# A gated linear recurrence followed by a token and channel mixer: the two chunks of a later group taken one after the other, with another table of urgencies

## The chip, the cores and the metric

The kernel runs on one core of a Trainium2 chip. The metric is the device time of one execution in microseconds (us), and lower is better. The engines are called as the profile calls them: PE is TensorE (PEld is its loading of weights, which can overlap the products), DVE is VectorE, ACT is ScalarE, POOL is GpSimd and SP is SyncE. POOL and SP only issue transfers in the part of the program that matters here.

## The reference

Two blocks run one after the other. The first is a recurrence with complex gates, for 4 batches, 8 heads, 768 positions and a head size of 48. The second mixes over positions at rank 32 and then over channels with a hidden width of 1536. All data are float32.

```python
mag = np.sqrt(a_re * a_re + a_im * a_im)
scale = np.minimum(mag, 0.999) / (mag + 1e-06)
ar, ai = a_re * scale, a_im * scale
for t in range(S):                         # S = 768
    S_re, S_im = (ar_t * S_re - ai_t * S_im + k_t v_t^T,
                  ar_t * S_im + ai_t * S_re)
    y[:, :, t] = q_t @ S_re
x = y as (B, S, H*D)                       # (4, 768, 384)
h = x.transpose(0, 2, 1) @ U @ V           # U (768, 32), V (32, 768)
u = x + h.transpose(0, 2, 1)
out = u + np.maximum(u @ w_ch1, 0) @ w_ch2 # w_ch1 (384, 1536), w_ch2 (1536, 384)
```

## The kernel before, in words

**Chunks.** The 4 x 768 positions are cut into 24 chunks of 128 (six to a batch). `GROUPS` holds chunks 0 and 1 as groups of one and then eleven groups of two (`GC = 2`). The gates (magnitude, logarithm, phase, sine and cosine) are worked out for a whole group at a time by `gates`, mostly on ACT and DVE. For each chunk, `prep` weighs q and k, turns them by their phases and transposes them on PE (`tr`, L660) into the tile `QK`, which has 96 rows.

**The chain of a chunk.** `chain(i)` makes the 128x128 causal matrix of each of the 8 heads level by level. There are five small steps on PE: three times `inner` (L694: 32 matmuls in tiles of the array that are 96 rows by 32 columns), then `corners` (L743: 16 matmuls, 96x32) and `corner` (L760: 8 matmuls, 96x64). In float32 each of these is two records in the trace, so one `inner` step shows as x64. Between two steps DVE multiplies `QK` in place (`times` and `grow`, recorded at L312, 96x1024) by totals of the gates (`T`). After each `inner` step a masked copy (`keep`, L700, DVE) takes the diagonal blocks out of PSUM into `DG`; four transfers by SP place them in `AT` (L731). ACT copies the corners into `AT` (L748, L764). Then come the transposes of k (`ks`, L780), the outputs (`yT`, L794 and, for all but the first chunk of a batch, L798), the state (`dk`, L809) and the turn back (`yr`, L824). `tot` (L578, in `gates`) and `yT` also use the array in tiles that are narrower than 128 columns.

**The mixer.** After the sixth chunk of a batch, three mixers (12 in all, two chunks each) are added to the plan: `mixed` (L861), `uTp` (L868), six steps `up` of 6 matmuls with 256 columns (L880), and the products `down` (L947; L904 for mixer 0). Results leave by POOL's queue (L891), those of the last mixer by SP's.

**The order.** Nothing is issued where it is written. Every step is added to a `Plan` with an engine, a cost, a rank, and what it reads and writes. `Plan.order` then lists all steps by simulating the engines with these costs, and this one list fixes each engine's order of instructions. A step with the lowest urgency among those that are ready goes first. The urgency of the steps of chunk i is looked up in the table `URGENCY` (`prep`, `levels` for the first three steps, `rest` for what follows); the mixers' large products have `n + 1000` and so fill what is left over. `way=1` marks PE steps that use tiles of the array: the planner charges `change` (0.12) where PE goes from one kind to the other, and prefers a step of the same kind if its urgency is within `stay` (4.0). Before the first mixer's products the planner puts `spare` matmuls (L1067), whose result nobody reads, where PE has nothing to do.

**Pairs.** For groups from `PAIRED = 6` on (chunks 10 to 23, seven groups), `chunks(g)` prepares both chunks and then calls `together` with both chains. `chain` is a generator that yields its five small steps; `together` takes the next one of each chain and adds the two as one PE step with the sum of the costs, the urgency of the first chunk, the reads of both, and PSUM tiles and destinations of both. Such a step shows as inner x128 in the trace. The chains' other steps are added between these, each with its own urgency.

Of the kernel before, what the change touches and what calls it, by code (L numbers as in the profile page):

```python
# [22 lines left out]
BLK = 32  # L23

URGENCY = {
    "w1": {0: -34.77, 1: -91.94, 2: 138.23, 3: 260.09, 4: 568.49, 5: 287.6, 6: 296.57},
    "w2": {0: 650.7, 2: 523.09, 4: -249.29, 6: 129.92, 8: 543.42, 10: 182.29, 12: 94.19},
    "gates": {0: -78.45, 1: -71.5, 2: 78.63, 4: -234.27, 6: 143.18, 8: 215.64, 10: 30.99, 12: 47.49, 14: 142.08,
        16: 274.38, 18: 114.7, 20: -16.24, 22: 169.1},
    "angles": {0: -70.73, 1: -53.23, 2: -131.01, 4: 19.06, 6: -65.31, 8: 37.85, 10: -61.12, 12: -16.54, 14: -136.88,  # L30
        16: -195.15, 18: 196.11, 20: -175.82, 22: 226.2},
    "prep": {0: -170.41, 1: 140, 2: -141.91, 3: 258.54, 4: -14.67, 5: -36.16, 6: -99.41, 7: -276.32, 8: 64.29,
        9: 195.98, 10: -226.17, 11: -71.5, 12: -336.86, 13: -82.47, 14: 72.82, 15: -103.91, 16: 99.41, 17: 10.29,
        18: -125.03, 19: 313.53, 20: -42.62, 21: 390.29, 22: -13.68, 23: -202.37},
    "levels": {0: 25.49, 1: -241.92, 2: 189.55, 3: -76.47, 4: -144.22, 5: -38.31, 6: -47.77, 7: -81.78, 8: 73.09,
        9: -35.34, 10: 106.7, 11: -81.83, 12: 144.3, 13: -3.44, 14: 138.61, 15: 149.75, 16: -3.41, 17: -279.49,
        18: 131.44, 19: 484.09, 20: 212.52, 21: -233.89, 22: -120.03, 23: 283.09},
    "rest": {0: 147.76, 1: 132.91, 2: 111.2, 3: 94.14, 4: 79.58, 5: 43.3, 6: 213.4, 7: 72.05, 8: 69.08, 9: 53.84,
        10: 15.71, 11: 8.04, 12: 146.3, 13: 334.57, 14: 62.95, 15: 59.48, 16: -119.25, 17: -34.74, 18: 266.96,
        19: 135.14, 20: 205.81, 21: 22.53, 22: 320.65, 23: -217.03},  # L40
}


# [129 lines left out]
def kernel(  # L173
# [37 lines left out]
    NCH = S // CH  # L211
# [3 lines left out]
    MC = 2  # L215
# [3 lines left out]

    GROUPS = [(0, 1), (1, 2)] + [(n, n + GC) for n in range(2, NT, GC)]  # L220
    NG = len(GROUPS)

    PAIRED = 6

    SIZES = (4, 8, 16, 32, 64, 128)
    NTOT = CH // 2
# [21 lines left out]
    def buffer(base, tag, bufs, shape, space=None, padded=None):  # L248

        if tag not in pools:  # L250
            pools[tag] = pool(tag, bufs, **({"space": space} if space else {}))
        plan.buffer(base, tag, bufs, space is not None)
        kw = {"padded_shape": padded} if padded else {}
        makers[base] = lambda: pools[tag].tile(shape, FP, tag=tag, name=base[0], **kw)

    def ring(base, tag, tiles):

        plan.buffer(base, tag, len(tiles))
        n = plan.turn[base] % len(tiles)
        makers[base] = lambda: tiles[n]  # L260
# [19 lines left out]
    def c_dma(n):  # L280
        return n * 512 / 170e3


    def PE(*a, **kw):
        plan.add("PE", *a, late=0.17, **kw)
# [34 lines left out]
    def where(i):  # L320
        return divmod(i, NCH)
# [16 lines left out]
    w1 = singles.tile([128, KD, FF], FP, name="w1")  # L338
    w2 = singles.tile([128, KF, DM], FP, name="w2")
# [87 lines left out]
    def load_qkv(i):  # L427
        buffer(("qk", i), "qk", 2, [128, 2, H, D])
        ring(("VP", i), "VP", VP)
        for u, src in enumerate((q, k)):  # L430
            SP(c_dma(DM), ("load", (1.3, 2.5)[i] if i < 2 else i + 3.7), lambda u=u, src=src: nc.sync.dma_start(out=get("qk", i)[:, u], in_=rows(src, i)),
               writes=[("qk", i, u)])
        SP(c_dma(DM), ("load", (1.4, 2.6)[i] if i < 2 else i + 4), lambda: nc.sync.dma_start(out=get("VP", i)[:, :, 0:D], in_=rows(v, i)), writes=[("VP", i)])
# [205 lines left out]
    def prep(i):  # L639
        R1 = "prep", i  # L640
        g = group_of(i)
        qk, QK = ("qk", i), ("QK", i)
        buffer(QK, "QK", 3, [D2, 2, H, CH])
        def weigh():
            a = get(*qk).rearrange("p u h d -> p u (h d)")
            mul(a, a, get("es", i))
        DVE(c_dve(2 * DM), R1, weigh, [("es", i)], [qk])
        for u in range(2):
            qkc = ("qkc", 2 * i + u)
            buffer(qkc, "qkc", 1, [128, H, 2, D])  # L650
            DVE(c_dve(2 * DM), R1, lambda u=u, qkc=qkc: mul(
                get(*qkc), get(*qk)[:, u].unsqueeze(2).to_broadcast([128, H, 2, D]), get("cs", g)[:, i - GROUPS[g][0]]),
                [qk, ("cs", g)], [qkc])
            for hh in range(2):
                ps = ("tr", (i, u, hh))
                psum(ps, "T", [128, HH, CH])

                def turn(qkc=qkc, hh=hh, ps=ps):
                    for j in range(HH):
                        nc.tensor.transpose(out=get(*ps)[0:D2, j], in_=get(*qkc)[:, hh * HH + j].rearrange("p u d -> p (u d)"),  # L660
                                            identity=ident)
                PE(0.44, R1, turn, [qkc], [ps], takes=[QK])
                ACT(c_act(HH * CH) - 0.05, R1, lambda u=u, hh=hh, ps=ps: nc.scalar.copy(  # L663
                    out=get(*QK)[:, u, hh * HH:(hh + 1) * HH], in_=get(*ps)[0:D2]), [ps], [QK + ((u, hh),)])
# [3 lines left out]
    def chain(i):  # L668
        c = where(i)[1]
        RL, RR = ("levels", i), ("rest", i)  # L670
        QK, DGi, ATi, VPi = ("QK", i), ("DG", i), ("AT", i), ("VP", i)
# [9 lines left out]
        def inner(n, hf):  # L681

            def part(a, p):
                return a if hf < 8 else a.rearrange(p + " (b x t) -> " + p + " b x t", x=2, t=hf)[..., 1, :]

            w = BLK if hf < 8 else BLK // 2
            ps = ("inner", (i, n))
            psum(ps, "A", [128, H, w], [128, 512 // w, w])

            def products():  # L690
                for h in range(H):
                    for j in range(CH // BLK):
                        js = slice(j * BLK, (j + 1) * BLK)
                        nc.tensor.matmul(out=get(*ps)[js, h], lhsT=k_of(h)[:, js], rhs=part(q_of(h)[:, js], "p"), start=True,  # L694
                                         stop=True, tile_position=(0, j * BLK))
            yield 0.6, RL, products, [QK], ps, DGi

            def keep():
                to, a = part(get(*DGi), "p h"), get(*ps)
                nc.vector.copy_predicated(out=to, mask=part(mask[:, n], "p").unsqueeze(1).to_broadcast(list(to.shape)),  # L700
                                          data=a if hf < 8 else a.rearrange("p h (b t) -> p h b t", t=hf))
            DVE(0.17 + 0.00104 * H * w, RL, keep, [ps, ("mask", 0)], [DGi])
# [15 lines left out]

            times(rank, hf, 2 * hf, hf, H * CH - hf, 0, u0, u1)

        yield from inner(5, 2)


        times(RL, 4, 16, 8, H * CH - 8, 0)
        yield from inner(1, 8)
        times(RL, 4, 16, 0, H * CH + 8, 2)
        grow(RL, 8)
        yield from inner(0, 16)
        for j in range(CH // BLK):
            js = slice(j * BLK, (j + 1) * BLK)  # L730
            SP(0.65, ("place", i), lambda js=js: nc.sync.dma_start(out=get(*ATi)[js, :, js], in_=get(*DGi)[js]), [DGi],  # L731
# [3 lines left out]
        ps1 = ("corners", i)  # L735
        psum(ps1, "A", [128, HH, BLK], [128, 4 * HH, BLK])

        def corners():
            for p in range(HH):
                for u in range(2):  # L740
                    for r in (0, 64):
                        h, to = 2 * p + u, r + u * BLK
                        nc.tensor.matmul(out=get(*ps1)[to:to + BLK, p], lhsT=k_of(h)[:, r:r + BLK],  # L743
                                         rhs=q_of(h)[:, r + BLK:r + 2 * BLK], start=True, stop=True, tile_position=(0, to))
        yield 0.4, RR, corners, [QK], ps1, ATi
        for r in (0, 64):
            for u in range(2):
                ACT(0.32, RR, lambda r=r, u=u: nc.scalar.copy(  # L748
# [4 lines left out]
        ps2 = ("corner", i)  # L753
        psum(ps2, "A", [128, HH, 64], [128, H, 64])

        def corner():
            for p in range(HH):
                for u in range(2):
                    h = 2 * p + u
                    nc.tensor.matmul(out=get(*ps2)[u * 64:(u + 1) * 64, p], lhsT=k_of(h)[:, 0:64], rhs=q_of(h)[:, 64:128],  # L760
                                     start=True, stop=True, tile_position=(0, u * 64))
        yield 0.5, RR, corner, [QK], ps2, ATi
        for u in range(2):
            ACT(0.37, RR, lambda u=u: nc.scalar.copy(  # L764
                out=get(*ATi).rearrange("p (a u) t -> p a u t", u=2)[0:64, :, u, 64:128], in_=get(*ps2)[u * 64:(u + 1) * 64]),
# [4 lines left out]
        if c < NCH - 1:  # L770
# [3 lines left out]
            for hh in range(2):  # L774
                ps = ("ks ps", (i, hh))
# [24 lines left out]
        for p0 in (0, 2):  # L800
            PE(0.95 if c else 0.5, RR, lambda p0=p0: outputs(p0), [VPi, ATi, QK] + ([("G", i - 1)] if c else []), [y + (p0,)], way=1,
               takes=[yTs])
# [203 lines left out]
    weights()  # L1006
    exps, trigs = "natural_log_exp_and_others", "trig_and_small"

    def together(chains):

        while True:
            at = [next(c, None) for c in chains]
            if at[0] is None:
                break
            cost, rank, f, reads, ps, to = zip(*at)
            PE(sum(cost), rank[0], lambda f=f: [x() for x in f], sum(reads, []), list(ps), way=1, takes=list(to))

    def chunks(g):
        both = list(range(*GROUPS[g]))
        for these in [both] if g >= PAIRED else [[i] for i in both]:  # L1020
            for i in these:
                load_qkv(i)
                prep(i)
            together([chain(i) for i in these])
            for i in these:
                if where(i)[1] == NCH - 1:
                    for m in range(i // MC - NCH // MC + 1, i // MC + 1):
                        mixer(m)


    waits, later, done = [], [], 0
    for g in range(NG):
        load_a(g)
        magnitudes, totals, turns, waves = gates(g)
        rank = "gates", GROUPS[g][0]
# [87 lines left out]
```

## Time and profile before

| | us |
|---|---|
| Median of 12 runs | 726.68 |
| Lowest and highest of them | 724.42, 728.17 |
| The profiled execution's own time | 727.8 |
| Its span, first to last instruction | 726.0 |

| engine | busy us | share of the span | instructions |
|---|---|---|---|
| PE | 707.7 | 97% | 10322 |
| PEld | 616.2 | 85% | 10322 |
| DVE | 484.0 | 67% | 732 |
| ACT | 399.3 | 55% | 734 |
| POOL | 49.8 | 7% | 91 |

The profiled execution's time is 1.8 us longer than its span and 1.1 us above the median of the runs. Matmuls are pipelined: each takes longer than the distance from its start to the start of the next, so that busy times of PE overlap, and the cost of a matmul to its successors is read from starts. `spare` makes up 58.5 us of PE's busy time.

### The profile page before, as it was taken

What the parts mean: (1) busy time and instruction counts of PE and PEld (TensorE: products, weight loads), DVE (VectorE), ACT (ScalarE), POOL (GpSimd) and SP (SyncE); (2) the same over time, 40 slices, a digit from 0 to 9 for tenths busy, and PEclk for the clock granted to TensorE, in tenths of its full rate; (3) what the DMA queues carried; (4) which work ended last, traced back from release to release, by engine and by line L of the source; (5) the groups of instructions that cost most, each with busy time, mean ns of one, the idle gap of its engine ahead of it and who ended that gap; (6) DMA issues with size and microseconds to landing.
All of it is one profiled execution on the core that took longest, in us unless ns stands there. A gap on an engine that the chain in (4) does not pass through costs nothing.

```text
span 726.0 us, 23175 instructions
## 1 busy us (share of the span) xinstructions
PE 707.7 (97%) x10322; PEld 616.2 (85%) x10322; DVE 484.0 (67%) x732; ACT 399.3 (55%) x734; POOL 49.8 (7%) x91
## 2 busy tenths in 40 slices
PE   7899998999999999999999999999999999999998
PEld 7777888786778888988888888798899898989997
DVE  5898999787997957878587686295684641322313
ACT  6695977857789686669988636514314122010010
POOL 5010000010100100000010001000000000000000
PEclk9999999999999999999999999999999999999999
DMA  8787854687415323253441042212110000000000
GB/s 204 154 210 145 203 105 81 136 197 129 101 32 115 67 60 65 43 106 63 84 96 23 17 91 55 45 30 44 34 38 14 13 28 1 22 1 23 6 16 23
DMA packets 165251, 53.00 MB, mean 73 GB/s; under 512 B 154080, under 2 KB 160416, under 8 KB 165152
## 3 DMA queue, kind: packets, MB, share of 16 engines
q1 hardware_dynamic: 161072, 42.26, 27.1%
q0 software_dynamic: 4080, 9.27, 5.5%
q8 instruction: 81, 1.33, 0.8%
q14 instruction: 18, 0.15, 0.1%
HBM read 33.59 MB, written 4.72 MB: 53 GB/s over the span
## 4 chain that ended last, share of the span: by engine, by line
PE 75%; ACT 11%; DVE 9%; issue 3%; DMA 1%; DVEq 0%; ACTq 0%
PE up L880 21%; PE down L947 19%; PE inner L694 5%; PE tr L660 5%; PE dk L809 3%; PE yT L794 3%; DVE QK L312 3%; ACT x L309 2%; PE down L904 2%; PE yT L798 2%; PE es ps L552 2%; PE mixed L861 2%; PE tot L578 2%; ACT y L309 1%; PE spare L1067 1%
## 5 line engine op out<-in xcount | busy, mean ns | idle before, releaser
L880 PE MATMUL up<-uT,w 128*128 128x256 f32 x864 | 196.1, 382 | 0.0
L312 DVE TENSOR_TENSOR QK<-QK,T 96x1024 f32<-96x1024 f32 x144 | 169.6, 1185 | 17.5 <-PE corners L743 7.2
L880 PEld LDWEIGHTS up<-uT,w 128*128 128x128 f32 x864 | 161.3, 190 | 22.8 <-issue 0.8
L309 ACT ACTIVATE h<-up 128x512 f32<-128x512 f32 x72 | 42.7, 594 | 158.2 <-PE up L880 155.6
L947 PE MATMUL down<-w,h 128*128 128x192 f32 x396 | 71.8, 327 | 0.0
L947 PEld LDWEIGHTS down<-w,h 128*128 128x128 f32 x396 | 65.2, 190 | 3.3
L312 DVE TENSOR_TENSOR qkc<-qk,cs 128x768 f32<-128x768 f32 x48 | 45.8, 953 | 30.2 <-PE tr L660 24.9
L939 DVE TENSOR_TENSOR stage<-h 128x384 f32<-128x384 f32 x22 | 12.2, 555 | 75.9 <-ACT h L309 75.9
L1067 PE MATMUL spare<-ident 128*128 128x128 f32 x404 | 58.5, 292 | 3.3 <-issue 1.9
L663 ACT COPY QK<-tr 96x512 f32<-96x512 f32 x96 | 52.1, 582 | 14.7 <-PE tr L660 14.5
L694 PEld LDWEIGHTS inner<-QK 96*32 96x32 f32 x4608 | 45.2, 109 | 17.4 <-issue 10.5
L1067 PEld LDWEIGHTS spare<-ident 128*128 128x128 f32 x404 | 52.4, 202 | 6.5 <-issue 2.7
L315 DVE TENSOR_TENSOR xo<-down,xo 128x192 f32<-128x192 f32 (+1 forms) x79 | 29.5, 385 | 38.2 <-PE down L947 38.2
L660 PE MATMUL tr<-ident,qkc 128*96 128x128 f32 x384 | 52.7, 275 | 2.0 <-DVE qkc L312 1.1
L694 PE MATMUL inner<-QK 96*32 96x16 f32 (+1 forms) x4608 | 50.7, 190 | 3.5 <-issue 2.8
L660 PEld LDWEIGHTS tr<-ident,qkc 128*96 128x96 f32 x384 | 41.3, 127 | 8.3 <-issue 1.8
L748 ACT COPY AT<-corners 32x128 f32<-32x128 f32 x96 | 24.5, 256 | 32.1 <-PE corners L743 31.0
L891 POOL DMA_DIRECT2D out_dram<-xo x32 | 17.9, 560 | 335.8 <-DVE xo L315 316.0
L700 DVE COPY_PREDICATED DG<-mask,inner 128x128 f32<-128x128 int32 (+1 forms) x72 | 24.2, 339 | 19.3 <-PE inner L694 19.0
L794 PE MATMUL yT<-AT,VP 128*64 128x128 f32 x384 | 36.8, 279 | 0.0
L947 PE MATMUL down<-stage 128*128 128x192 f32 x198 | 36.4, 327 | 0.0
L306 ACT ACT_TABLE_LOAD x26 | 33.4, 1283 | 1.2 <-PEq L1107 0.7
(116 smaller groups left out, 1106.7 us busy)
## 6 DMA issues: line engine op xcount, KB each, us to landing
stage<-in_moe_w_ch_dram SPq DMA_DIRECT2D x12, 768.0 KB, 5.1
ar<-in_a_re_dram SPq DMA_DIRECT2D x24, 192.0 KB, 3.4
ai<-in_a_im_dram SPq DMA_DIRECT2D x24, 192.0 KB, 3.7
qk<-in_q_dram SPq DMA_DIRECT2D x24, 192.0 KB, 3.3
qk<-in_k_dram SPq DMA_DIRECT2D x24, 192.0 KB, 4.4
VP<-in_v_dram SPq DMA_DIRECT2D x24, 192.0 KB, 3.2
w<-stage POOLq DMA_DIRECT2D x12, 384.0 KB, 6.6
T<-E SPq DMA_DIRECT2D x44, 96.0 KB, 3.2
```

The source lines that it names most:

```text
L306: ACT(1.37, rank, lambda: nc.scalar.preload_act_table_set(name), writes=[TABLE])
L309: return nc.scalar.activation(out=o, in_=i, func=f, **kw)
L312: nc.vector.tensor_tensor(out=o, in0=a, in1=b, op=OP.mult)
L315: nc.vector.tensor_tensor(out=o, in0=a, in1=b, op=OP.add)
L660: nc.tensor.transpose(out=get(*ps)[0:D2, j], in_=get(*qkc)[:, hh * HH + j].rearrange("p u d -> p (u d)"), identity=ident)
L663: ACT(c_act(HH * CH) - 0.05, R1, lambda u=u, hh=hh, ps=ps: nc.scalar.copy(out=get(*QK)[:, u, hh * HH:(hh + 1) * HH], in_=get(*ps)[0:D2]), ...
L694: nc.tensor.matmul(out=get(*ps)[js, h], lhsT=k_of(h)[:, js], rhs=part(q_of(h)[:, js], "p"), start=True, stop=True, tile_position=(0, j * BLK))
L748: ACT(0.32, RR, lambda r=r, u=u: nc.scalar.copy(out=get(*ATi).rearrange("p (a u) t -> p a u t", u=2)[r:r + BLK, :, u, r + BLK:r + 2 * BLK] ...
L794: nc.tensor.matmul(out=a[u * DP:(u + 1) * DP, p], lhsT=vv[:, h], rhs=get(*ATi)[:, h], start=True, stop=(c == 0), tile_position=(0, u * DP))
L880: nc.tensor.matmul(out=get(*ps)[:, e], lhsT=w1[:, f, (ff + e) * 128:(ff + e + 1) * 128], rhs=get(*uT)[:, f], start=(f == 0), stop=(f == KD ...
L947: nc.tensor.matmul(out=get(*to)[:, part], lhsT=x(j), rhs=y[:, j], start=(first and j == 0), stop=(j == KH - 1), skip_group_check=not first)
L1067: nc.tensor.matmul(out=spare[0], lhsT=ident, rhs=ident, start=True, stop=True)
```

## The change

The pairs are taken out: `PAIRED` and `together` go, `chain` adds each of its five small steps by itself, as a PE step with its own urgency, and `chunks` goes through the chunks of a group one after the other. For groups 2 to 5 that is what was done before, since there `together` had one chain. All seven tables in `URGENCY` have other numbers. The instructions that are issued are the same ones in kind and number; their order changes.

```diff
 URGENCY = {
-    "w1": {0: -34.77, 1: -91.94, 2: 138.23, 3: 260.09, 4: 568.49, 5: 287.6, 6: 296.57},
+    "w1": {0: 95.68, 1: -114.1, 2: 119.35, 3: 318.09, 4: 584.75, 5: 240.49, 6: 274.57},
...
-    "levels": {0: 25.49, 1: -241.92, 2: 189.55, 3: -76.47, 4: -144.22, 5: -38.31, 6: -47.77, 7: -81.78, 8: 73.09,
+    "levels": {0: 36.28, 1: -163.69, 2: 90.75, 3: -118.68, 4: -103.74, 5: 8.67, 6: -52.01, 7: -23.82, 8: 96, 9: 43.86,
...
-    PAIRED = 6
-
...
-            yield 0.6, RL, products, [QK], ps, DGi
+            PE(0.6, RL, products, [QK], [ps], way=1, takes=[DGi])
...
-        yield from inner(5, 2)
+        inner(5, 2)
...
-        yield from inner(1, 8)
+        inner(1, 8)
...
-        yield from inner(0, 16)
+        inner(0, 16)
...
-        yield 0.4, RR, corners, [QK], ps1, ATi
+        PE(0.4, RR, corners, [QK], [ps1], way=1, takes=[ATi])
...
-        yield 0.5, RR, corner, [QK], ps2, ATi
+        PE(0.5, RR, corner, [QK], [ps2], way=1, takes=[ATi])
...
-    def together(chains):
-
-        while True:
-            at = [next(c, None) for c in chains]
-            if at[0] is None:
-                break
-            cost, rank, f, reads, ps, to = zip(*at)
-            PE(sum(cost), rank[0], lambda f=f: [x() for x in f], sum(reads, []), list(ps), way=1, takes=list(to))
-
     def chunks(g):
-        both = list(range(*GROUPS[g]))
-        for these in [both] if g >= PAIRED else [[i] for i in both]:
-            for i in these:
-                load_qkv(i)
-                prep(i)
-            together([chain(i) for i in these])
-            for i in these:
-                if where(i)[1] == NCH - 1:
-                    for m in range(i // MC - NCH // MC + 1, i // MC + 1):
-                        mixer(m)
+        for i in range(*GROUPS[g]):
+            load_qkv(i)
+            prep(i)
+            chain(i)
+            if where(i)[1] == NCH - 1:
+                for m in range(i // MC - NCH // MC + 1, i // MC + 1):
+                    mixer(m)
```

More of the change, by code (lines that the diff above doesn't have):

```diff
@@ L25 @@
 URGENCY = {
-    "w1": {0: -34.77, 1: -91.94, 2: 138.23, 3: 260.09, 4: 568.49, 5: 287.6, 6: 296.57},
[L27 to L31, printed above, removed]
@@ L32 @@
-    "prep": {0: -170.41, 1: 140, 2: -141.91, 3: 258.54, 4: -14.67, 5: -36.16, 6: -99.41, 7: -276.32, 8: 64.29,
-        9: 195.98, 10: -226.17, 11: -71.5, 12: -336.86, 13: -82.47, 14: 72.82, 15: -103.91, 16: 99.41, 17: 10.29,
-        18: -125.03, 19: 313.53, 20: -42.62, 21: 390.29, 22: -13.68, 23: -202.37},
-    "levels": {0: 25.49, 1: -241.92, 2: 189.55, 3: -76.47, 4: -144.22, 5: -38.31, 6: -47.77, 7: -81.78, 8: 73.09,
-        9: -35.34, 10: 106.7, 11: -81.83, 12: 144.3, 13: -3.44, 14: 138.61, 15: 149.75, 16: -3.41, 17: -279.49,
-        18: 131.44, 19: 484.09, 20: 212.52, 21: -233.89, 22: -120.03, 23: 283.09},
@@ L38 @@
-    "rest": {0: 147.76, 1: 132.91, 2: 111.2, 3: 94.14, 4: 79.58, 5: 43.3, 6: 213.4, 7: 72.05, 8: 69.08, 9: 53.84,
-        10: 15.71, 11: 8.04, 12: 146.3, 13: 334.57, 14: 62.95, 15: 59.48, 16: -119.25, 17: -34.74, 18: 266.96,
-        19: 135.14, 20: 205.81, 21: 22.53, 22: 320.65, 23: -217.03},
+    "w1": {0: 95.68, 1: -114.1, 2: 119.35, 3: 318.09, 4: 584.75, 5: 240.49, 6: 274.57},
+    "w2": {0: 491.44, 2: 430.31, 4: -244.92, 6: 252.33, 8: 503.62, 10: 122.04, 12: 198.27},
+    "gates": {0: -36.9, 1: -11.04, 2: 97.92, 4: -176.1, 6: 172.63, 8: 170.19, 10: 39.76, 12: 33.76, 14: 86.36,
+        16: 212.52, 18: 142.25, 20: -14.92, 22: 119.88},
@@ new lines @@
+    "angles": {0: -48.49, 1: -68.04, 2: -149.7, 4: 26.37, 6: -18.74, 8: 27.33, 10: 2.93, 12: -18.2, 14: -106.29,
+        16: -135.42, 18: 99.1, 20: -223.01, 22: 213.99},
+    "prep": {0: -120.66, 1: 125.67, 2: -144.48, 3: 213.93, 4: -34.4, 5: 6.43, 6: -98.93, 7: -166.15, 8: 67.48,
+        9: 198.22, 10: -212.51, 11: 47.76, 12: -241.36, 13: -15.05, 14: 36.41, 15: -84.27, 16: 57.48, 17: 29.52,
+        18: -106.17, 19: 297.29, 20: 8.87, 21: 340.29, 22: 15.55, 23: -177.02},
+    "levels": {0: 36.28, 1: -163.69, 2: 90.75, 3: -118.68, 4: -103.74, 5: 8.67, 6: -52.01, 7: -23.82, 8: 96, 9: 43.86,
+        10: 78.26, 11: -98.96, 12: 174.48, 13: 49.88, 14: 84.4, 15: 102.2, 16: 22.96, 17: -168.27, 18: 153.18,
+        19: 552.85, 20: 149.19, 21: -218.14, 22: -98.92, 23: 245.11},
@@ L41 @@
+    "rest": {0: 160.12, 1: 84.71, 2: 92.21, 3: 84.11, 4: 44.14, 5: 13.55, 6: 221.57, 7: 36.88, 8: 6.37, 9: 42.74,
+        10: 3.06, 11: -2.44, 12: 170.29, 13: 268.3, 14: 86.43, 15: 53.53, 16: -130.49, 17: -80.04, 18: 187.27,
+        19: 178.6, 20: 234.63, 21: 84.11, 22: 252.98, 23: -194.62},
 }
```

## The prediction

> **What bounds the kernel now.** I read the page first, then busy time by stretch, then PE's waits, and last PE's instructions in order of time.
>
> ```profile
> PE 707.7 (97%) x10322; PEld 616.2 (85%) x10322; DVE 484.0 (67%) x732; ACT 399.3 (55%) x734; POOL 49.8 (7%) x91
> ...
> PE   7899998999999999999999999999999999999998
> ...
> PEclk9999999999999999999999999999999999999999
> ```
>
> PE is busy in nearly all of every slice but the first two, at its full clock. A busy PE may still hide slack, so the next view matters more: each row below is a stretch, its length, and the busy time of PE, PEld, DVE, ACT and POOL.
>
> ```profile
> 0.00:145.00 145.00, 132.74 (x2449) 113.90 (x2450) 125.60 (x186) 110.62 (x203) 16.56 (x40) 0.99 0.70 155
> ...
> 181.00:300.00 119.00, 117.53 (x2171) 100.22 (x2171) 100.04 (x139) 91.95 (x168) 8.68 (x13) 1.00 0.35 74
> 300.00:400.00 100.00, 99.62 (x1605) 86.19 (x1605) 73.93 (x109) 82.69 (x139) 6.40 (x10) 1.00 0.33 69
> 400.00:500.00 100.00, 98.99 (x1628) 86.92 (x1628) 66.09 (x99) 44.85 (x97) 5.77 (x9) 1.00 0.23 49
> 500.00:606.00 106.00, 106.00 (x1666) 95.59 (x1665) 58.83 (x93) 30.60 (x72) 3.24 (x6) 1.00 0.11 24
> 606.00:726.00 120.00, 116.77 (x634) 106.98 (x632) 31.77 (x70) 13.76 (x24) 4.86 (x9) 1.00 0.04 14
> ```
>
> Until 145 us DVE and ACT feed a PE that fills its gaps with spare matmuls. From 181 to 606 us PE stands idle for 119.00 - 117.53, 0.38, 1.01 and 0 us: 2.9 us in 425. From 606 us on only mixer products are left. So the end is set by the sum of PE's work; DVE, the next busiest, has 19 of 119 us free in its worst stretch and 47 of 106 in the last. PE's waits from 181 us on say the same (total, times, longest):
>
> ```profile
> PE inner L694 <- issue: 1.6, 3, 0.7
> PE tr L660 <- DVE qkc L312: 0.9, 1, 0.9
> PE uTp L868 <- DVE xo L315: 0.2, 1, 0.2
> ```
>
> No paired step is seen to wait for a chunk that is late. Something that shortens waits has 2.9 us to win; something that lengthens PE's own work is paid in full.
>
> **The instructions** are the same in kind and number: 5519 on PE in both built orders, 202 spares among them, 734 on DVE, 736 on ACT. The change's description speaks also of seven down products, of two banks and of last outputs by SP; both kernels have these, and the last 67 rows of PE's built order are equal. What remains is order. PE's first 200 rows are equal too, and row 200 stands at 181 us, so the start on PE is carried over. On DVE the first difference is a masked copy (0.29 us) set ahead of a multiplication at 90 us, on ACT a swap of two squares at 175 us. I take them at 0; the spares cover the first, and without that cover it is worth 0.3 us either way.
>
> **What a visit to the tiles costs.** In this view (start, duration, line, operation, number of records) starts count, since durations overlap:
>
> ```profile
> 476.13 1.14 PE L947 MATMUL down<-w,h 128*128 128x192 f32 x6
> 477.20 1.30 PE L694 MATMUL inner<-QK 96*32 96x16 f32 x128
> 478.43 1.08 PE L660 MATMUL tr<-ident,qkc 128*96 128x128 f32 x8
> 479.34 1.14 PE L947 MATMUL down<-w,h 128*128 128x192 f32 x6
> 480.32 2.11 PE L947 MATMUL down<-stage,h 128*128 128x192 f32 x12
> ```
>
> Six down records followed by more of them take 480.32 - 479.34 = 0.98 us; the six before the pair's inner step take 477.20 - 476.13 = 1.07. Going to the tiles costs 0.09. The joint step takes 478.43 - 477.20 = 1.23 for 128 records. A step of one chunk:
>
> ```profile
> 196.23 0.81 PE L552 MATMUL es ps<-GL,mid 128*128 128x384 f32 x2
> 196.96 0.69 PE L578 MATMUL tot<-total,GL 128*64 128x64 f32 x16
> 197.58 0.74 PE L694 MATMUL inner<-QK 96*32 96x16 f32 x64
> 198.25 0.69 PE L578 MATMUL tot<-total,GL 128*64 128x64 f32 x16
> ```
>
> It takes 198.25 - 197.58 = 0.67. Two of them make 1.34, or 0.11 over the joint step: that is the price of leaving a tile shape once, here for another shape (128x64), and the joint step's own exit to the full array is inside its 1.23. So a visit that is split in two pays 0.09 + 0.11 = 0.20 more.
>
> **How many.** The change dissolves 35 joint steps (7 groups, 5 steps) into 70. If each stood alone this would cost 35 x 0.20 = 7.0 us. The planner keeps tiled steps together when their urgencies lie close, so I counted in the built orders from PE's row 200 on, leaving out the alternation inside yT, which is the same in both. Stretches of tiled steps: 66 before, 76 after. Changes from one tiled kind of step to another inside a stretch: 18 before, 42 after (inner next to tot, corner next to inner, yT next to inner, each of another chunk). So 10 x 0.20 = 2.0 us for stretches, and 24 changes of shape. For these the view has 0.11 (inner to tot); between yT and inner it is up to 0.20, and between two shapes of equal width about 0.05. Most of the 24 have inner on one side, so I take 0.10: 2.4 us, with 1.2 and 4.8 as ends. Sum: 4.4 us more of PE's own time, from 3.2 to 6.8.
>
> On this the Trainium skill has a rule that speaks against the change: TensorEngine Tiling (Array Packing), section Key Properties, says that a change of tiling mode drains TensorE and that a change of tile within a mode does not. TensorE: Matmul & The Clock Gate, section Single matmul latency, gives a matmul's fixed part as 398 cycles, 166 ns at full clock; as an estimate, a full drain at each of the 44 changes would be 7.3 us, giving 734.0. The rows show about 0.1 us per change, and they decide.
>
> **Waits.** Gone with the pairs is the demand that both chunks' QK be ready, and the run of 128 small matmuls in which the trace has its gaps of issue (1.6 us in three; one of them, though, inside a step of one chunk). All of the 2.9 us is the most that this can give back. New is closeness. I added up PE's work between successive steps of one chunk in both orders. A step's products end, DVE makes the masked copy (0.34 to 0.45 us) and the multiplication of QK (1.19), then the next step may start: 1.6 us at least, and twice the DVE work for a pair. After 181 us the order before has one distance under 2.2 us; its pairs have at least 3.1 for corners to corner, and 4 to 11 between inner steps. The order after has eleven under 2.2 (1.2 to 2.2 us), three of them before 300 us, where DVE is 84% busy. The PE instruction queue stops at such a step, and all the mixer products queued behind it stop too. A DVE step of 0.55 to 0.95 us queued ahead would make each late by up to about 0.45 us: 0 to 5 us. I set this against the gaps given back and take 0 for the sum of both, from -2.9 to +5.0.
>
> **Queues that are moved past.** On SP, four transfers that place DG now stand between the four transfers of T at several places, so T waits for a masked copy; on POOL three or four z transfers come in a row, behind outputs that wait for DVE. T feeds the multiplications, z the phase product (ph), and ph has no wait after 181 us in the list above. I count nothing; uncovered, it adds to the same 0 to 5 us. After the last small tiled step both built orders have the same 117 us of mixer products (by row durations), so the end is unchanged.
>
> **The sum.** The profiled execution's 727.8 us + 4.4 + 0 = 732.2 us. That execution lies 1.1 us above the median of the runs, so the median to expect is 731.1.
>
> **Rivals.**
> *Coupling given back (faster).* Each chunk goes ahead when its own QK is ready, and PE's idle time after 181 us vanishes. With the changes of tiling at no cost this is 726.7 - 2.9 = 723.8 us. It decides if a change costs under 0.04 us (44 x 0.04 = 1.8, leaving a gain of 1.1). The views speak against it: paired steps are not seen waiting for data, and every change costs 0.09 or more. With the changes at the low end, 3.2 - 2.9, it lands at 727.0, which counts as no change.
> *Closeness (slower still).* All eleven near steps wait: 731.1 + 5.0 = 736.1, more if a late T or z adds. For it: DVE's 84%. Against: near distances lie beyond 300 us too, where DVE has 26% or more free.
> *PE has slack.* PEld is 85% busy, and then 4 us would vanish: 726.7. The Trainium skill, in Perfetto Trace Analysis, section Identifying the Most-Contended Engine, takes that share and not matmul busy time as the measure of headroom; by it some 110 us would be open. Against it stands the down step above: 0.98 / 6 = 0.163 us from start to start with nothing waited for; its weights load ahead.
>
> **How the numbers follow.** About 0.2% (1.5 us) is what a measurement of this kernel can tell from no change. The forecast (729 to 734 us) has 0.62; closeness or dearer changes (over 734) 0.22; waits given back or slack, 728.1 to 729 us, 0.03; within 725.2 to 728.1, 0.09; faster 0.04. So slower 0.87, same 0.09, faster 0.04. The range 727.0 to 735.5 leaves out the free changes below and the fullest closeness above.
>
> **What would show it.** Right: records of spare unchanged at 404, up starting near 145.6 us, inner as x64 in more visits with 0.67 us each, PE's idle time after 181 us near 3 us, and the mixer-only end starting 4 us later, near 610 us. Wrong: PE waits on DVE QK of several us (closeness), on ph (queues), an earlier start of the end stretch (coupling), or a start that moved before 181 us.

## The result, and the profile after

The kernel after takes 729.91 us (median of 12 runs, 728.06 to 731.76), the kernel before 726.51 us in the runs beside it. The ratio is 1.0046, with a 95% interval from 1.0033 to 1.0059: slower by 0.46%, or 3.4 us. The profiled execution after took 729.9 us and has a span of 728.0 us, 2.0 us more than the span shown before.

Busy times on the page of the kernel after:

```profile
PE 711.9 (98%) x10322; PEld 618.1 (85%) x10322; DVE 484.3 (67%) x732; ACT 399.7 (55%) x734; POOL 49.5 (7%) x91
```

The work is the same and PE is busy 4.2 us longer. The stretches (length, then the busy time of PE, PEld, DVE, ACT, POOL) say where:

```profile
0.00:145.00 145.00, 133.11 (x2450) 113.97 (x2451) 125.86 (x186) 111.24 (x203) 16.59 (x40) 0.99 0.70 156
...
181.00:300.00 119.00, 118.76 (x2206) 101.52 (x2205) 102.06 (x139) 94.84 (x173) 7.56 (x11) 1.00 0.36 74
300.00:400.00 100.00, 99.63 (x1870) 85.20 (x1870) 79.88 (x117) 75.96 (x138) 5.85 (x9) 1.00 0.38 78
400.00:500.00 100.00, 99.89 (x1787) 86.44 (x1776) 72.42 (x104) 54.28 (x107) 4.80 (x7) 1.00 0.21 43
500.00:606.00 106.00, 106.00 (x1199) 96.06 (x1199) 44.55 (x77) 24.64 (x56) 4.86 (x9) 1.00 0.08 20
```

The start is as it was. From 181 to 606 us PE stands idle for 0.24 + 0.37 + 0.11 + 0 = 0.7 us, where it was 2.9. PE's waits from 181 us on are these two:

```profile
PE ph L608 <- ACT QK L661: 0.2, 1, 0.2
PE tr L658 <- ACT x L307: 0.2, 1, 0.2
```

So PE waits less and still ends later, with the same work: it has become slower at it. PE in order of time (start, duration), after:

```profile
301.65 0.62 PE L822 MATMUL yr<-ident,yTs 128*128 128x128 f32 x4
302.20 0.76 PE L692 MATMUL inner<-QK 96*32 96x32 f32 x64
302.89 1.08 PE L658 MATMUL tr<-ident,qkc 128*96 128x128 f32 x8
...
306.80 1.31 PE L692 MATMUL inner<-QK 96*32 96x32 f32 x128
308.04 1.56 PE L550 MATMUL es ps<-GL,mid 128*128 128x384 f32 x4
```

An inner step of one chunk alone takes 0.69 us; where the planner sets two side by side (x128), they take 1.24 together.

**A ledger of PE's time.** I added up the distances from one start to the next of all PE records in each trace, from the first up to the last record. A *change* is a passage between the full array, tiles of 64 columns (corner, tot, yT) and tiles of 32 (inner, corners, rank); its price is what the distance has over the step's own spacing. In all traces the medians are the same: 0.093 us from the full array to either width, 0.095 to 0.100 from 64 columns to the full array or to 32, 0.104 to 0.117 from 32 to 64 or to the full array, and nothing between two steps of the same width, though one has 96 rows and the other 128. A second cost sits behind it: after an exit to the full array the second record, too, comes late, by 0.104 us (up, down, ph, mixed) or 0.035 to 0.057 (transposes, dk). *Waits* are distances over 0.15 us beyond all that.

| kernel | changes | first up to end, us | changes, us | second records | waits | rest |
|---|---|---|---|---|---|---|
| before | 154 | 576.8 | 15.6 | 5.7 | 4.4 | 551.2 |
| after | 189 | 579.2 | 19.4 | 6.4 | 2.1 | 551.3 |
| before_again | 154 | 576.0 | 15.6 | 5.6 | 3.6 | 551.2 |
| after_again | 189 | 578.7 | 19.4 | 6.4 | 1.5 | 551.4 |
| pairs_other_table | 154 | 585.9 | 15.6 | 6.0 | 11.1 | 553.2 |
| single_old_table | 202 | 586.1 | 20.4 | 7.1 | 6.2 | 552.5 |
| full_ahead | 161 | 583.8 | 16.3 | 6.3 | 2.5 | 551.0 + 7.8 |
| full_between | 224 | 593.6 | 22.8 | 9.2 | 2.5 | 551.3 + 7.8 |
| shifted | 154 | 581.3 | 15.6 | 5.7 | 8.8 | 551.2 |
| after_shifted | 189 | 578.6 | 19.4 | 6.4 | 1.6 | 551.4 |
| single_fewer | 173 | 578.6 | 17.2 | 6.4 | 3.2 | 551.8 |
| fewer_changes | 141 | 572.4 | 13.9 | 5.5 | 2.5 | 550.5 |

The rest, PE's own work, is equal to 0.2 us between before and after. The change adds 3.8 us of changes and 0.7 us of second records and gives back 2.3 us of waits (2.1 by the second pair of profiles). From the first up to the end the two pairs of traces differ by 2.4 and 2.7 us, of the measured 3.4.

Up to 1 us is not in the ledger, and the granted clock is the likely place of it. In both first traces the clock is halved for 3.4 us, at 60.1 us before and at 59.6 us after; in the second pair it is full throughout up to the last product, and the first up comes 2.8 and 2.3 us sooner. All 12 runs of the kernel after have a clock of 0.995 to 0.999. The 49 runs of the kernel before beside the experiments have 1.000 in 19 cases, with a median of 725.1 us, and 0.998 or less in 29, with 727.3. Against the latter the kernel after is 2.6 us slower, as in the ledger; that this is the whole of it isn't shown.

### The profile page after: what moved, and what is told of

Read it like the earlier page. It is cut to its first block, busy times and chain, and to the rows that moved or that the text cites. A ratio compares the mean times of both kernels' runs of the same rounds, so it can differ in the third digit from the quotient of the medians.

```text
span 728.0 us, 23185 instructions
## 1 busy us (share of the span) xinstructions
PE 711.9 (98%) x10322; PEld 618.1 (85%) x10322; DVE 484.3 (67%) x732; ACT 399.7 (55%) x734; POOL 49.5 (7%) x91
## 3 DMA queue, kind: packets, MB, share of 16 engines
q8 instruction: 81, 1.33, 0.8%
## 4 chain that ended last, share of the span: by engine, by line
PE 72%; ACT 4%; issue 2%; DVE 2%; DMA 1%; POOL 0%; POOLq 0%
PE up L878 23%; PE down L945 20%; PE inner L692 5%; PE tr L658 4%; PE dk L807 3%; PE yT L792 2%; PE yT L796 2%; PE mixed L859 2%; PE down L902 2%; PE es ps L550 2%; PE ph L608 1%; PE ks ps L778 1%; DMA w<-stage 1%; PE corner L758 1%; PE tot L576 1%
## 5 line engine op out<-in xcount | busy, mean ns | idle before, releaser
L310 DVE TENSOR_TENSOR QK<-QK,T 96x1024 f32<-96x1024 f32 (+1 forms) x144 | 169.5, 1185 | 7.1 <-PE corners L741 4.9
L310 DVE TENSOR_TENSOR qkc<-qk,cs 128x768 f32<-128x768 f32 x48 | 45.7, 953 | 19.4 <-PE tr L658 12.9
L692 PE MATMUL inner<-QK 96*32 96x16 f32 (+1 forms) x4608 | 53.8, 190 | 2.0 <-issue 1.4
L945 PEld LDWEIGHTS down<-stage 128*128 128x128 f32 x198 | 32.5, 190 | 0.5
```

Source lines behind the costliest of these rows:

```text
L310: nc.vector.tensor_tensor(out=o, in0=a, in1=b, op=OP.mult)
L945: nc.tensor.matmul(out=get(*to)[:, part], lhsT=x(j), rhs=y[:, j], start=(first and j == 0), stop=(j == KH - 1), skip_group_check=not first)
```

## The experiments

**The two parts by themselves: pairs or not, and which table.** `pairs_other_table` is the kernel before with the table of the kernel after, `single_old_table` the kernel after with the table of the kernel before:

```diff
 # pairs_other_table; the other way round in single_old_table
 URGENCY = {
-    "w1": {0: -34.77, 1: -91.94, 2: 138.23, 3: 260.09, 4: 568.49, 5: 287.6, 6: 296.57},
+    "w1": {0: 95.68, 1: -114.1, 2: 119.35, 3: 318.09, 4: 584.75, 5: 240.49, 6: 274.57},
...
```

> The kernel before with the urgency table of the kernel after; the pairs stay. In its built order PE changes the width of its tiles (full array, 64 or 32 columns) 154 times from the first up on, as often as in the kernel before (154) and 35 times less than in the kernel after (189). Theory (each change costs PE about 0.10 us, and the pairs set their number): 726.5 us, like the kernel before, within 1.5. Rival (the table moves the waits and makes the difference): about 729.9, like the kernel after.

Measured: 738.46 us, ratio 1.0143 [1.0117, 1.0169] to the kernel before (727.88 beside it). Both theories missed. The count of changes came out as built and priced (154, 15.6 us), but the ledger has 11.1 us of waits. The page's waits of PE from 181 us on come to 8.0 us, where the kernel before has 2.7; the largest are:

```profile
PE yT L794 <- ACT AT L764: 2.3, 1, 2.3
PE corner L760 <- DVE QK L312: 1.7, 1, 1.7
PE inner L694 <- issue: 1.1, 2, 0.8
PE tot L578 <- DVE uT L870: 1.1, 1, 1.1
PE corners L743 <- DVE QK L312: 1.0, 1, 1.0
...
```

The same kernel around the largest of them, DVE, PE and ACT:

```profile
308.77 2.36 DVE L312 TENSOR_TENSOR QK<-QK,T 96x1024 f32<-96x1024 f32 x2
...
311.28 1.15 PE L760 MATMUL corner<-QK 96*64 96x64 f32 x32 [1.74 <-DVE QK L312]
...
313.52 1.50 ACT L764 COPY AT<-corner 64x256 f32<-64x256 f32 x4
...
314.68 0.69 PE L794 MATMUL yT<-AT,VP 128*64 128x128 f32 x2 [2.25 <-ACT AT L764]
```

The joint corner step waits for two multiplications of 1.18 us each, one for each chunk, and the next step for four copies on ACT. This is the coupling of the pair: between these steps this order gives PE nothing else to do. Such waits for a pair's data (yT, corner and corners) are 5.0 us.

Not all of the rest is waiting. The row of this stretch (its third number from the end is the granted clock) shows 0.97:

```profile
300.00:400.00 100.00, 91.89 (x1574) 77.72 (x1573) 74.30 (x105) 73.17 (x132) 6.09 (x9) 0.97 0.35 71
```

The clock was halved for 6.8 us from 312.7 us on, while PE stood still: the eight steps of yT from 314.68 us take 4.14 us, the next eight, from 324.21, take 1.91. The ledger counts part of this as waits and part as rest. Another 6.8 us at half clock, from 124.9 us, go with a first up at 149.0 us in place of 145.6. All six runs have a clock of 0.988 to 0.993, those of the kernel before beside them 0.992 to 1.000. So the 10.6 us are waits and lost clock; how much of the latter the waits bring about, no run separates. The table matters by that, and not by the count of changes.

> The kernel after with the urgency table of the kernel before; the pairs are gone. Its built order has 202 changes of width, 48 more than the kernel before. Theory: 726.5 + 48 x 0.10 = 731.3 us, from 729 to 733 with waits given back or added. Rival (the table makes the difference): 726.5.

Measured: 736.37 us, ratio 1.0116 [1.0093, 1.0139]. The rival is out, and my range of 729 to 733 us was too low. The 48 changes cost 4.8 us and second records 1.4, 1.4 us more than expected; waits rose by 1.8 us on the trace before, and the rest by 1.3 us, for which I have no cause. So a change costs about the same 0.1 us with either table.

The two parts do not add up: each alone costs 8.5 to 10.6 us, both together 3.4. With the table of the kernel after, it is keeping the pairs that is dear (738.46 us against 729.91).

**The price of a change, by itself.** A matmul of the full array goes into each of the 35 joint steps, once ahead and once between the halves; the planner sees the same costs, so that all else keeps its order:

```diff
+            def full(p):
+                a = get(*p)
+                w = a.shape[-1]
+                nc.tensor.matmul(out=a[:, 0:128 // w], lhsT=ident, rhs=ident.rearrange("p (a b) -> p a b", b=w), start=True, stop=True)
+
+            def both(f=f, ps=ps):
+                for n, x in enumerate(f):
+                    if len(f) == 2 and n == 1:      # full_ahead: n == 0
+                        full(ps[n])
+                    x()
-            PE(sum(cost), rank[0], lambda f=f: [x() for x in f], sum(reads, []), list(ps), way=1, takes=list(to))
+            PE(sum(cost), rank[0], both, sum(reads, []), list(ps), way=1, takes=list(to))
```

> The kernel before with one more matmul of the full array (128 columns, its result is overwritten) ahead of each of the 35 joint steps; the planner's order is the same. 35 x 0.22 us (two records of 0.11, as in spare) = 7.8 us of products, and 161 changes of width in place of 154, 0.7 us: 735.0 us. Rival (PE has slack): 726.5.

> The same 35 matmuls, set between the two chunks' halves of each joint step, so that PE leaves the tiles and comes back: 224 changes of width, 63 more than with the matmuls ahead. Theory: 63 x 0.10 = 6.3 us over the run with the matmuls ahead, about 741.3. By the Trainium skill, TensorE: Matmul & The Clock Gate, section Single matmul latency (0.166 us for a full drain), it would be 10.5 us over it, 745.5. Rival (PE has slack): no difference between the two.

Measured: 734.39 us ahead, ratio 1.0083 [1.0054, 1.0111]; 743.76 us between, ratio 1.0216 [1.0183, 1.0250]. PE has no slack: in both, the added matmuls are paid for (ahead, 6.5 us in time; the ledger has 7.8 of products, 0.7 of changes and 0.6 of second records more, and 1.9 of waits less). The difference is 9.4 us, more than the 6.3 expected and less than 10.5. The same step in both traces, ahead first and then between:

```profile
471.21 0.81 PE L861 MATMUL mixed<-r,V 128*128 128x384 f32 x2
471.86 0.38 PE L1020 MATMUL inner<-ident 128*128 128x128 f32 x2
472.17 1.32 PE L694 MATMUL inner<-QK 96*32 96x32 f32 x128
473.42 0.55 PE L868 MATMUL uTp<-ident,xo 128*128 128x128 f32 x3
```

```profile
478.67 0.81 PE L861 MATMUL mixed<-r,V 128*128 128x384 f32 x2
479.41 0.76 PE L694 MATMUL inner<-QK 96*32 96x32 f32 x64
480.11 0.49 PE L1020 MATMUL inner<-ident 128*128 128x128 f32 x2
480.52 0.76 PE L694 MATMUL inner<-QK 96*32 96x32 f32 x64
481.22 0.55 PE L868 MATMUL uTp<-ident,xo 128*128 128x128 f32 x3
```

Ahead, the full matmul's two records take 472.17 - 471.86 = 0.31 us (0.22 and one change); between, 480.52 - 480.11 = 0.41. The 0.10 us more is the second record, which I had not seen. With it the ledger says 6.5 + 2.9 = 9.4 us for the difference, as measured.

**A second profile of each kernel.**

> The kernel before, unchanged, for a second profile. In the profile before, PE stood still inside inner steps at 242.5, 313.9 and 420.4 us (0.64, 0.57, 0.95 us from start to start), each 1.6 to 2.0 us after the start of a 16 KB instruction transfer. Theory (PE has used up its instructions and waits for that transfer; the place is set by the program, the length by the transfer): gaps at the same records, with lengths that differ by some tenths; some may vanish. Rival (chance events): gaps at other records.

> The kernel after, unchanged, for a second profile. Theory: the same 189 changes of width at 0.09 to 0.12 us, waits from the first up on near 2.1 us, no gap of issue over 0.5 us after 181 us, since none of its 16 KB boundaries falls badly in a run of inner matmuls. Rival: gaps as in the kernel before.

Measured: 724.21 and 727.04 us, one run each. In the kernel before, the waits inside inner steps are at the same three records (0.38, 0.57, 0.37 us beyond the spacing where it was 0.63, 0.56, 0.94); in the kernel after there are again none of 0.5 us after 181 us. So they belong to the program, and their length varies. The start up to the first up was 2.8 and 2.3 us shorter than in the first pair, in both kernels, without the half clock near 60 us: it adds scatter and not the difference.

**Moving PE's instructions by half a block.** The page counts 81 transfers of instructions for 1.33 MB, 16 KB each. In the first trace each of the three waits lay 1.6 to 2.0 us after the start of one. Both kernels get 32 small matmuls at the start, which PE does where it waits anyway. With their loads of weights these are 128 instructions, half a block as an estimate (1.33 MB over the page's 20,644 records of PE and PEld make about 64 bytes each):

```diff
         if not spare:
             spare.append(pools["psM"].tile([128, 128], FP, tag="psM", name="spare", padded_shape=[128, 512]))
+            for n in range(32):
+                js = slice(n % 4 * BLK, (n % 4 + 1) * BLK)
+                nc.tensor.matmul(out=spare[0][js, 0:BLK], lhsT=ident[0:D2, js], rhs=ident[0:D2, 0:BLK],
+                                 start=True, stop=True, tile_position=(0, n % 4 * BLK))
```

> The kernel before with 32 matmuls of the inner kind (64 records, 0.6 us, result not read) ahead of the first spares, where PE waits for 1.7 us afterwards; the rest of the order is the same. The 16 KB boundaries of PE's instructions then fall half a block earlier in the work. Theory: the gaps inside inner at 242.5, 313.9 and 420.4 us leave these places, others may come up where a boundary now falls inside a run of small matmuls; the time within 2 us of the kernel before. Rival (the gaps belong to these inner steps, by their data): they stay at the same inner steps.

Measured: 732.55 us, ratio 1.0096 [1.0060, 1.0132]; the bound of 2 us was missed by far. PE's waits from 181 us on in the kernel before, shifted:

```profile
PE inner L694 <- issue: 2.3, 3, 1.0
PE tot L578 <- issue: 1.6, 1, 1.6
...
PE yT L798 <- issue: 0.7, 1, 0.7
PE tr L660 <- issue: 0.6, 1, 0.6
```

One of them, in the same trace:

```profile
427.11 1.19 PE L694 MATMUL inner<-QK 96*32 96x16 f32 x119
429.31 0.27 PE L694 MATMUL inner<-QK 96*32 96x16 f32 x9 [1.01 <-issue]
```

No step with a pair's data stands still as such: all three gaps are gone (behind the step that had the one at 313.9 us, yr now waits 0.3 us for ACT's copy of yTs), and others are in new places, all but one of them 1.2 to 1.7 us after the start of a transfer. The order and the changes are the same as before, and waits went from 4.4 to 8.8 us. As I read it, PE runs out of instructions where many small matmuls follow each other, and where the block ends decides how long. The ends of the gaps speak for it: the twelve traces have 19 idle gaps by issue of over 0.3 us after 143 us, and each of them ends 2.2 to 2.6 us after a transfer of instructions has begun, though these begin about 9 us apart on average.

> The kernel after with 32 matmuls of the inner kind ahead of the first spares (as in the run shifted), so that the 16 KB boundaries of PE's instructions fall half a block earlier in the work. The same shift cost the kernel before 4.4 us of waits in the trace. Theory (waits of issue are set by where the boundaries fall, and the kernel after as it is has few by chance): waits from the first up on rise from 2.1 us to 3 to 8, and the time by as much, 731 to 736 us. Rival (without pairs the runs of small matmuls are too short to use up a block): waits stay near 2 us, the time within 1 us of 729.9.

Measured: 728.18 us, ratio 1.0033 [1.0013, 1.0054], and waits of 1.6 us. My theory was wrong here and the rival nearly right: without pairs, in this order, neither place of the blocks makes PE wait for instructions after the first up. So it is not by one lucky placement that the change gives waits back. How much it gives back does depend on the placement, and the sign of the result with it: under the shift the ledger has 8.8 us of waits with pairs and 1.6 without, and the kernel without pairs is the faster one, with 1.0033 where the kernel with pairs has 1.0096 of the time of the kernel before. Yet the lack is one of density and not of pairs alone: `single_old_table` has four such gaps after 181 us, two of them in runs of 128 records that the planner made of two single inner steps.

**Fewer changes.** If changes are the price, an order with fewer should gain. Two more tables were made with the count of changes in the built order as a guide, one for pairs and one for single chunks:

```diff
 # fewer_changes, in the kernel before; single_fewer likewise in the kernel after
 URGENCY = {
...
-    "gates": {0: -78.45, 1: -71.5, 2: 78.63, 4: -234.27, 6: 143.18, 8: 215.64, 10: 30.99, 12: 47.49, 14: 142.08,
-        16: 274.38, 18: 114.7, 20: -16.24, 22: 169.1},
+    "gates": {0: -78.45, 1: -71.5, 2: 78.63, 4: -522.07, 6: 147.24, 8: -70.52, 10: 60.32, 12: 34.12, 14: 872.6, 16: 509.81, 18: 192.33, 20: -43.68, 22: 579.65},
...
```

> The kernel before (pairs kept) with another urgency table, chosen for few changes of width in the built order: 141 from the first up on in place of 154, 65 of them exits to the full array in place of 70. Theory: 13 x 0.105 + 5 x 0.08 (the second record after an exit is late too) = 1.8 us less, 724.8 us, if waits stay as they are (1 us either way). Rival (waits by the new order decide): anything from 724 to 732.

Measured: 723.51 us, ratio 0.9957 [0.9938, 0.9977]: faster than both kernels, and 3.4 us under the median of the kernel before beside it (726.94), where 1.8 was expected. The ledger shows 1.7 us less for changes, 0.1 to 0.2 for second records, 1 to 2 us less waiting than in the two traces of before, and 0.7 less of rest.

> The kernel after (no pairs) with an urgency table chosen for fewer changes of width in the built order: 173 from the first up on in place of 189, 74 exits to the full array in place of 77. Theory (it is the number of changes that costs, not that chunks go one by one): 16 x 0.105 + 3 x 0.08 = 1.9 us less than the kernel after, 1.5 us more than the kernel before, about 728.0 us where the kernel before has 726.5; waits 1 us either way. Rival (chunks taken singly cost by waiting for DVE, however they are ordered): no gain, 3.4 us over the kernel before.

Measured: 729.61 us, ratio 1.0051 [1.0031, 1.0070]: no gain over the kernel after. The trace has 2.2 us less for changes, near what was expected, but 1.7 us more of waits than `after_again` (yr behind DVE's G, 0.7 us, and two gaps of issue of 0.4). Of the rival's cause, waiting for DVE, this one wait of 0.7 us is all, and no multiplication of QK is in it. So the number of changes is not enough by itself; an order that joins more small steps makes PE wait elsewhere.

## Why the prediction was right, and where its steps were off

The sign, the main mechanism (dearer changes of tiles on a PE without slack) and the range held: 731.1 us was forecast, 729.91 measured; +4.4 us was the forecast difference, +3.4 the measured one. That the two are so close is partly luck: two errors in the sum cancel, and the waits given back, for which I took 0, are made up for in part by the 1 us that the ledger does not hold. And with the instruction blocks half a block further on, the sign would have been the other one; the forecast had no term for where a block ends.

*The start and the end* were equal, as read from the order: the first up at 145.2 us after 145.6, 404 records of spare in both, and 117.0 us from the last tile of yT to the last product in both. The mixers' last stretch began 2.0 us later, not 4.

*The price of a change* was right: 0.09 in, 0.11 out, and about 0.1 between widths. The 0.20 (yT and inner) and 0.05 (equal width) that I gave beside it are whole distances; less the step's own spacing they are 0.10 and 0.

*The number* was too high. I took 10 stretches twice and 24 changes inside them, 44 in all. By width there are 35: 7 stretches more (70 exits to the full array, then 77) and 21 changes inside them. I had let corner next to yT or tot count, which costs nothing (both 64 columns wide; 0.05 us from start to start, as inside corner), and had taken rank for a step of the full array, though it uses 32 columns; a rank next to an inner step is no change.

*The second record* was missing from the sum: 0.7 us. The two errors cancel nearly, by luck: 4.4 us forecast, 3.8 + 0.7 = 4.5 in the trace.

*The waits* are the term that was mis-sized. I set what the change gives back against what closeness takes and wrote 0; the traces show -2.3 and -2.1 us. So PE's idle time after 181 us was 0.7 us and not near 3, and the end began 2 us later and not 4. PE waited for no multiplication of QK in the kernel after, though eleven distances were under 2.2 us: no wait came of them. And I had read the gaps of issue as something to be had back in part only, with the argument that one was inside a single chunk's step; the kernel after has none in either placement that was run.

*The rivals.* "PE has slack" is refuted by `full_ahead`. "Coupling given back" had a gain of about 2 us right, but not its cause: what went are the gaps of issue (1.6 us) and one wait of tr for qkc (0.9), and not waits for a pair's later chunk. It fell because a change costs 0.1 us and not under 0.04. "Closeness" did not appear in the kernel after, though `pairs_other_table` shows that another table can bring 5 us of waits for a pair's data.

*The rule on draining* in TensorEngine Tiling (Array Packing), section Key Properties, agrees with the traces in that a change of width costs PE about 0.1 us; that PE drains in this time, no run shows. Here the mode that counts is the width in columns; 96 and 128 rows at 64 columns mix at no cost (yT's two kinds follow each other at their own spacing). The estimate of 0.166 us a drain was too high for each change; with the second record an exit comes to 0.13 to 0.22.

## What to carry to other kernels

Where PE sets the end, count in the built order how often it changes the width of its tiles, and price each from starts of records, the second record after an exit included; putting like steps of independent work side by side saves 0.22 to 0.31 us for each visit to the tiles that goes away. Then look at what the joining does: a joint step waits for the later of its inputs, and a long run of tiny matmuls can use up the instructions that have been fetched. A table of priorities made for one structure is no baseline for another: the same pairs cost 10.6 us more with the other table. And a difference of 3 us in a program like this one is checked with the instructions moved by half a block: here that alone cost one kernel 5.6 us and turned the order of the two.

## What the runs showed of the hardware that I had not expected

After an exit from tiles to the full array the second record is late as well, by 0.104 us with 192 to 384 columns, in all twelve traces. A change between steps of 96 and of 128 rows is free if both have 64 columns (0.05 us from corner to yT or to tot, which is corner's own spacing).

PE stands still for 0.4 to 1.7 us in or right behind runs of small matmuls (about 9 ns from start to start in inner), 1.2 to 2.4 us after a 16 KB transfer of instructions has begun in all but one case, and goes on 2.2 to 2.6 us after that beginning in all 19; in the kernel before, at the same records in two executions. Half a block of instructions at the start moved these places and cost one kernel 4 us of waits, and the other nothing. That the fetch is late is inferred from when the transfers start; a kernel with its blocks laid out to avoid it was not tried.
